# A split last PV, a maximum taken away inside PSUM and spare matmuls in the tail of a fused attention and soft-MoE kernel

## The chip, the cores and the metric

The kernel runs on one core of a Trainium2 chip. The metric is the device time in microseconds of one execution; of the runs of a kernel the median counts. A profile belongs to one execution and has a span, from the first to the last recorded instruction, that is a little shorter than that execution's time.

## What is computed

Two stages follow each other. The first is attention with a choice of key chunks, for 4 batches, 8 heads, 768 positions and a head width of 64:

```
ub   = sum_d max(q * k_min[chunk], q * k_max[chunk])    # 24 chunks of 32 keys, causal
sel  = the 6 chunks of each query with the largest ub
attn = softmax(q k^T / 8 over chosen, causal keys);  x = attn v     # -> [3072, 512]
```

The second is a soft mixture of experts over all 3072 tokens, with 8 experts of 4 slots each (32 slots):

```
logits = x phi
d = softmax of logits over the tokens;  slot_input = d^T x
slot_out[e] = relu(slot_input[e] w1[e]) w2[e]           # w1: 512 x 1024, w2: 1024 x 512
c = softmax of logits over the slots;   out = c slot_out
```

## The kernel before

**Work and order.** The order of the instructions on each engine is written out by hand. A loop over `i` goes through 16 pairs of heads, four pairs to a batch, in a software pipeline: in turn `i` it makes scores and exponentials of pair `i` (`scores`, `expo`, six groups of key blocks), chooses chunks for pair `i + 1`, loads and transposes pairs ahead, multiplies probabilities with values for pair `i - 1` (`pv`, in parts `[0, 1, 2]`, `[3]`, `[4]`, `[5]`, one number for each tile of 128 queries), and normalises and transposes the result of pair `i - 2` (`normalise`, `x_transposes`, `evac_x`). `expo` runs ScalarE's exponential (L289) and then a mask select on GpSimd (POOL, L291).

**The MoE part beside it.** When a batch's four pairs are through, `moe_logits` multiplies the transposed x with phi, `moe_copy` and `moe_max` take the largest logit of each slot over the tokens, `moe_bound` and `moe_exp` bring it to all partitions and take it away, and the running maximum `m_run` and the running sums `si_acc` are corrected by `dm`. `moe_comb` makes the softmax over the slots (`c_pad`), `moe_dispatch` the slot inputs (`si`), and `moe_ct` transposes `c`.

**Weights.** The 16 blocks of expert weights, 1 MB each, are loaded by GpSimd's queue (`load_w`, L120) in the turns that `wplan` (L456 to L461) names: none in turns 2, 5, 8 and 11, two in 12 and 13, one elsewhere. Values of pair `i + 2` (L132) stand just ahead of them in the queue, mask selects just behind.

**The tail.** Behind the loop come L546 to L677. PV of the last pair is done as `[0, 1, 2, 3]` and `[4, 5]`, into two tiles of the pool `p_sc`, and normalised in the same two pieces (L549 to L562); the pair's x is copied out by ScalarE for the first piece and by VectorE for the second. The logits of the last batch are accumulated in one PSUM tile, three quarters of the width before the last pair is ready, one quarter after it. `moe_copy` (L360) reduces them to `pm`, L370 transposes that, L377 reduces it to `mb`, L383 brings it to all partitions by a product with the identity in float32, L390 to L392 make the new maximum and subtract it, L396 takes the exponential, L427 is dispatch. L580 and L587 put the sums into the padded expert input `siT_pad` and the normaliser row `zrow`. `experts_in` (L605) and `experts_out` (L640) run four experts at once in four column groups of TensorE, `relu` and `hidden_T` stand between them. `normalisers` (L623 to L631) makes 24 column sums of `c` and the slot normaliser, between the halves of `experts_out`. L657 scales the expert output into `so_sb`. Then 24 tiles of output are made (L668), copied in turn by VectorE (L670) and ScalarE (L672), and written by SyncE's queue in pairs of tiles; the first and the last pair are written tile by tile.

**Pools of PSUM.** `p_sc` and `p_tp` have two buffers each, `p_at` one; a tile waits until the earlier user of its buffer has been read.

Of the kernel before, what the change touches and what calls it, by code (L numbers as in the profile page):

```python
# [46 lines left out]
def kernel(  # L47
# [247 lines left out]
        st["e", i, g] = e  # L295

    def pv(i, ts):
        if i == LAST and ts[0] in (0, 4):
            st["at", i] = p_sc.tile([P, 2, 512], F32, name="at_ps", tag="sc")
        elif ts[0] == 0:  # L300
            st["at", i] = p_at.tile([P, 2, 512], F32, name="at_ps", tag="at")
        at = st["at", i]
        for t in ts:
            for h in range(2):
                o = at[:, h, t * (D + 1):(t + 1) * (D + 1)]
                for kg in range(t + 1):
                    g, c = BLOCK[(kg, t)]
                    nc.tensor.matmul(  # L308
                        o, lhsT=st["e", i, g][:, h, c:c + P], rhs=v_t[i % NV][:, h, kg, :],
                        start=(kg == 0), stop=(kg == t),  # L310
                    )

    def normalise(i, t0=0, t1=NQT, at=None):
        b, j = divmod(i, NPB)
        at = st.pop(("at", i)) if at is None else at
        at = at[:, :, :NQT * (D + 1)].rearrange("p h (t d) -> p h t d", t=NQT)[:, :, t0:t1]
# [21 lines left out]
    def evac_x(i, t0=0, t1=NQT, copy=nc.vector.tensor_copy):  # L338
        b, j = divmod(i, NPB)
        ps = st.pop(("xTps", i, t0))  # L340
        copy(st["xT", b][:, j, t0 * P:t1 * P], ps[:, t0:t1].rearrange("p t c -> p (t c)"))


    def moe_logits(b, hgs=range(NDG), home=(p_tp, "tp")):
        if hgs[0] == 0:
            st["lgps", b] = home[0].tile([P, NQT, NS], F32, name="lg_ps", tag=home[1])
        ps, xT = st["lgps", b], st["xT", b]
        for t in range(NQT):
            for hg in hgs:
                nc.tensor.matmul(  # L350
                    ps[:, t, :], lhsT=xT[:, hg, t * P:(t + 1) * P], rhs=phi_sb[:, hg, :],
                    start=(hg == 0 and t == 0), stop=(hg == NDG - 1 and t == NQT - 1),
                )

    def moe_copy(b):
        lg = small.tile([P, NQT, NS], F32, name="lg", tag="lg")
        pm = small.tile([P, NS], F32, name="pm", tag="pm")
        ps = st.pop(("lgps", b))
        if b == B - 1:
            nc.vector.tensor_reduce(pm, ps.rearrange("p t s -> p s t"), axis=AX.X, op=ALU.max)  # L360
            nc.scalar.copy(lg, ps)
        else:
            nc.vector.tensor_copy(lg, ps)
            nc.vector.tensor_reduce(pm, lg.rearrange("p t s -> p s t"), axis=AX.X, op=ALU.max)
        st["lg", b], st["pm", b] = lg, pm

    def moe_max(b):
# [12 lines left out]
    def moe_exp(b):  # L380
        lg = st["lg", b]
        bc = p_tp.tile([P, NS], F32, name="bc_ps", tag="tp")
        nc.tensor.matmul(  # L383
            bc, lhsT=st.pop(("mb", b)).broadcast_to([NS, P]), rhs=identf[:NS, :NS], start=True, stop=True,
        )
# [10 lines left out]
        nc.scalar.activation(d_sb, ld, func=ACT.Exp)  # L396
        st["d", b] = d_sb
        if b > 0:

            dm = small.tile([P, 1, NS], F32, name="dm", tag="dm")  # L400
            nc.vector.tensor_tensor(dm[:, 0, :], m_old, m_new, op=ALU.subtract)
            nc.scalar.activation(dm, dm, func=ACT.Exp)
            if b == B - 1:
                moe_comb(b)
# [42 lines left out]
    def have(i):  # L447
        return 0 <= i < NPAIR
# [5 lines left out]


    wplan = {i: 1 for i in range(-1, NPAIR)}  # L456
    for i in (2, 5, 8, 11):
        wplan[i] = 0
    for i in (12, 13):
        wplan[i] = 2  # L460
    nw = 1  # L461

    def weights(i):
# [5 lines left out]
    for i in range(-2, NPAIR):  # L469
# [34 lines left out]
        if have(i - 2):  # L504
            x_transposes(i - 2)
        if have(i - 1):
            pv(i - 1, [3])
        if have(i + 2):
            transposes(i + 2, "q")
            evac_T(i + 2, "q")  # L510
# [10 lines left out]
        if have(i):  # L521
            scores(i, 4)
            expo(i, 4)
            scores(i, 5)
            expo(i, 5)
        if have(i + 1) and i >= 0:
            ns_transposes(i + 1)
            evac_ns(i + 1)
        if have(i - 1):
            pv(i - 1, [4])  # L530
        moe(moe_dispatch, i - 3)
        if have(i - 1):
            pv(i - 1, [5])
        if have(i + 2):
            qsplit(i + 2)
# [10 lines left out]
    pads = ctx.enter_context(tc.tile_pool(name="pads", bufs=1))  # L546
    siT_pad = pads.tile([P, NDG, E, CH], BF16, name="siT_pad")
    hT_pad = pads.tile([P, NFG, E, CH], BF16, name="hT_pad")
    normalise(LAST - 1)  # L549
    pv(LAST, [0, 1, 2, 3])  # L550
    at_a = st["at", LAST]
    x_transposes(LAST - 1)
    evac_x(LAST - 1, copy=nc.scalar.copy)
    normalise(LAST, 0, 4, at_a)
    pv(LAST, [4, 5])
    moe_logits(B - 1, range(NDG - 1), (p_at, "at"))
    x_transposes(LAST, 0, 4)
    evac_x(LAST, 0, 4, nc.scalar.copy)
    normalise(LAST, 4, NQT)
    x_transposes(LAST, 4, NQT)  # L560
    evac_x(LAST, 4, NQT)
    moe_logits(B - 1, range(NDG - 1, NDG))  # L562
    nc.gpsimd.memset(siT_pad, 0.0)
    nc.gpsimd.memset(hT_pad, 0.0)
    i_ctx.close()
    moe_copy(B - 1)
    moe_max(B - 1)
    moe_bound(B - 1)
    moe_exp(B - 1)
    moe_dispatch(B - 1)  # L570


    tail = ctx.enter_context(tc.tile_pool(name="tail", bufs=1))
# [11 lines left out]
    for g in range(2):  # L585
# [6 lines left out]
    moe_ct(B - 1)  # L592
# [30 lines left out]
    def normalisers():  # L623
        ps = p_tp.tile([P, B * NQT + 1], F32, name="cs_ps", tag="tp")
        for n in range(B * NQT):
            nc.tensor.matmul(
                ps[:, n:n + 1], lhsT=cT[:, n // 2, n % 2], rhs=ones_sq[:, :1], start=True, stop=True)
        nc.tensor.matmul(
            ps[:, B * NQT:], lhsT=zrow.rearrange("p j s -> p (j s)"), rhs=identf[:1, :1], start=True, stop=True)
        nc.vector.reciprocal(zinv, ps[:, B * NQT:])  # L630
        nc.vector.reciprocal(cinv, ps[:, :B * NQT])  # L631

    so_ps = p_at.tile([P, 2, 512], F32, name="so_ps", tag="at")

    def experts_out(f):
        for g in range(2):
            for fg in range(f * 4, (f + 1) * 4):
                for j in range(4):
                    e = g * 4 + j
                    nc.tensor.matmul(  # L640
                        so_ps[j * CH:(j + 1) * CH, 0, :], lhsT=hT_pad[:, fg, e, :],
                        rhs=w_sb[E + e][:, fg * Dm:(fg + 1) * Dm],
                        start=(g == 0 and fg == 0), stop=(g == 1 and fg == NFG - 1),
                    )

    experts_in(0, 0)
    experts_in(0, 1)
    relu(0)
    experts_in(1, 0)
    hidden_T(0)  # L650
    experts_in(1, 1)
    relu(1)
    experts_out(0)
    hidden_T(1)
    normalisers()
    experts_out(1)
    nc.scalar.activation(so_sb, so_ps[:, 0, :], func=ACT.Copy, scale=zinv)  # L657


# [2 lines left out]
    for m in range(B * NQT // 2):  # L662
        o_sb = op.tile([P, 2, Dm], F32, name="o_sb", tag="o_sb")
        rows = out[m * 2 * P:(m + 1) * 2 * P, :].rearrange("(p x) d -> p x d", x=2)
        for x in range(2):
            pool, tag = homes[n % 5]
            o_ps = pool.tile([P, Dm], F32, name="o_ps", tag=tag)
            nc.tensor.matmul(o_ps, lhsT=cT[:, m, x], rhs=so_sb, start=True, stop=True)  # L668
            if x == 0:
                nc.vector.tensor_scalar_mul(o_sb[:, x, :], o_ps, cinv[:, n:n + 1])  # L670
            else:
                nc.scalar.activation(o_sb[:, x, :], o_ps, func=ACT.Copy, scale=cinv[:, n:n + 1])  # L672
# [35 lines left out]
```

## Time and profile before

| what | value |
|---|---|
| three runs | 177.64, 177.72, 176.17 us; median 177.64 |
| the profiled execution | 177.53 us, span 175.8 |
| busy: TensorE, VectorE, ScalarE, GpSimd | 139.1, 128.8, 120.0, 99.9 us |
| weight blocks, issue to landing | 12.9 us median; the last is issued at 129.11 and lands 18.9 us later |
| output transfers | 6.29 MB through SyncE's queue, 14 issues |

In the page, section 2 cuts the span into 40 slices; a digit is the busy share in tenths, and `PEclk` is the clock that TensorE was granted, in tenths of full. The chain of work that ended last is followed back from the last instruction, each step to what released it. In the timeline a row gives start, length, engine, line, operation, tiles, shape, count, and in brackets the idle time before it and what ended it. PEld is the weight load that belongs to a matmul and can run ahead of it.

### The profile page before, as it was taken

The page shows a single profiled execution, that of the slowest core. Times are in us where ns is not written, and L with a number is a line of the kernel's source. Part 1 is how long each engine was busy: PE and PEld are TensorE (multiplying, and loading weights), DVE is VectorE, ACT ScalarE, POOL GpSimd, SP SyncE. Part 2 cuts the span into 40 slices and gives each one's busy share as a digit, 9 for nine tenths or more (in the row PEclk, how much of TensorE's full clock was granted, in tenths as well). Part 3 has the DMA queues.
Part 4 walks back from the last instruction along what each step waited for, and adds up shares of the span by engine and source line. Part 5 has one row for each costly group of instructions (what it writes and reads, how often), then busy time and mean ns, then how long its engine had stood idle before and what let it go on. Part 6 is the DMA issues. An engine that isn't in the chain of part 4 may idle for free.

```text
span 175.8 us, 5994 instructions
## 1 busy us (share of the span) xinstructions
PE 139.1 (79%) x2486; PEld 95.9 (55%) x2486; DVE 128.8 (73%) x429; ACT 120.0 (68%) x163; POOL 99.9 (57%) x194
## 2 busy tenths in 40 slices
PE   0449888999889889999988999999689569986500
PEld 0334556777567657766765776677467444532000
DVE  4456979999889998999998999999752650246530
ACT  2336798989789778988977698897667321156430
POOL 7995679869768557877775585759344600000000
PEclk9999999999999999999999999999999956999755
DMA  3999999999999999999999999199999993009995
GB/s 50 167 158 180 194 206 200 206 197 209 179 212 193 215 185 143 200 172 203 172 147 203 169 207 141 17 187 211 200 214 214 213 215 72 4 13 403 402 405 212
DMA packets 40460, 32.92 MB, mean 187 GB/s; under 512 B 26353, under 2 KB 34545, under 8 KB 40433
## 3 DMA queue, kind: packets, MB, share of 16 engines
q0 software_dynamic: 38416, 26.25, 101.8%
q1 hardware_dynamic: 2016, 6.29, 9.1%
q8 instruction: 19, 0.31, 0.7%
q14 instruction: 9, 0.07, 0.1%
HBM read 52.49 MB, written 6.29 MB: 334 GB/s over the span
## 4 chain that ended last, share of the span: by engine, by line
PE 36%; ACT 19%; DVE 13%; DMA 12%; POOL 11%; issue 5%; POOLq 0%; DVEq 0%; ACTq 0%
ACT e_sb L289 13%; DMA k_in<-in_k_dram 7%; PE sc_ps L271 6%; DMA out_dram<-o_sb 5%; PE at_ps L308 5%; PE sc_ps L277 4%; PE tr_ps L184 3%; PE h_ps L605 3%; DVE x_sb L321 3%; POOL e_sb L291 3%; POOL q_in L127 2%; PE ns_ps L253 2%; POOL k_in L127 2%; PE so_ps L640 2%; PE si_ps L427 2%
## 5 line engine op out<-in xcount | busy, mean ns | idle before, releaser
L289 ACT ACTIVATE e_sb<-sc_ps 128x1024 bf16<-128x1024 f32 x96 | 83.6, 936 | 10.9 <-PE sc_ps L277 9.9
L291 POOL TENSOR_SCALAR_AFFINE_SELECT e_sb<-e_sb 128x256 bf16<-128x256 bf16 x96 | 39.5, 423 | 32.7 <-ACT e_sb L289 32.0
L271 PE MATMUL sc_ps<-qT,kT 64*128 64x512 bf16 (+3 forms) x256 | 39.6, 310 | 6.6 <-ACT e_sb L289 6.3
L277 PE MATMUL sc_ps<-nsT,smask 64*128 64x512 bf16 (+3 forms) x256 | 36.8, 306 | 0.0
L308 PE MATMUL at_ps<-v_t,e_sb 128*128 128x65 bf16 x672 | 29.4, 194 | 1.2 <-DVE x_sb L321 1.1
L308 PEld LDWEIGHTS <-e_sb 128*128 128x128 bf16 x672 | 25.1, 98 | 3.4 <-DVE x_sb L321 1.6
L271 PEld LDWEIGHTS <-kT 64*128 64x128 bf16 x256 | 15.8, 94 | 16.8 <-issue 8.7
L242 DVE MAX8 mx<-ub_ps 128x8 f32<-128x24 f32 x192 | 18.8, 170 | 4.6 <-PE ub_ps L231 4.5
L202 DVE TENSOR_REDUCE mm<-kT 128x24 bf16<-128x768 bf16 x16 | 15.2, 949 | 4.0 <-ACT kT L193 4.0
L132 POOL DMA_DIRECT2D v_t<-in_v_dram x16 | 16.7, 1042 | 1.9 <-PE ns_ps L253 1.2
L193 ACT COPY kT<-tr_ps 128x768 bf16<-128x768 bf16 x16 | 12.8, 803 | 6.5 <-PE tr_ps L184 6.5
L321 DVE TENSOR_TENSOR x_sb<-at_ps,inv 128x768 bf16<-128x768 f32 (+2 forms) x17 | 15.5, 910 | 0.6
L277 PEld LDWEIGHTS <-smask 64*128 64x128 bf16 x256 | 13.1, 95 | 4.4 <-issue 0.3
L208 DVE TENSOR_REDUCE mm<-kT 128x24 bf16<-128x768 bf16 x16 | 15.1, 942 | 0.0
L193 ACT COPY qT<-tr_ps 128x768 bf16<-128x768 bf16 x16 | 13.2, 825 | 2.7 <-PE tr_ps L184 2.7
L184 PE MATMUL tr_ps<-ident,k_in 128*64 128x128 bf16 x192 | 9.2, 237 | 6.6 <-DMA k_in<-in_k_dram 5.5
L670 DVE TENSOR_SCALAR o_sb<-o_ps,cinv 128x512 f32<-128x512 f32 x12 | 8.6, 748 | 7.2 <-PE o_ps L668 4.1
L231 PE MATMUL ub_ps<-bd,qpn 128*128 128x48 bf16 x192 | 10.4, 187 | 2.8 <-DVE qpn L218 2.5
L127 POOL DMA_DIRECT2D k_in<-in_k_dram x16 | 11.7, 729 | 1.3 <-POOLq L692 0.8
L261 DVE COPY nsT<-ns_ps 128x768 bf16<-128x768 bf16 x16 | 8.9, 556 | 4.0 <-PE ns_ps L253 3.5
L672 ACT ACTIVATE o_sb<-o_ps,cinv 128x512 f32<-128x512 f32 x12 | 7.8, 688 | 5.7 <-DMA out_dram<-o_sb 3.8
L127 POOL DMA_DIRECT2D q_in<-in_q_dram x16 | 11.5, 721 | 0.0
(95 smaller groups left out, 213.2 us busy)
## 6 DMA issues: line engine op xcount, KB each, us to landing
w_sb<-in_moe_w_dram POOLq DMA_DIRECT2D x16, 1024.0 KB, 12.9
out_dram<-o_sb SPq DMA_DIRECT2D x10, 512.0 KB, 5.5
k_in<-in_k_dram POOLq DMA_DIRECT2D x16, 192.0 KB, 7.9
q_in<-in_q_dram POOLq DMA_DIRECT2D x16, 192.0 KB, 8.1
v_t<-in_v_dram POOLq DMA_DIRECT2D x16, 192.0 KB, 9.3
out_dram<-o_sb SPq DMA_DIRECT2D x4, 256.0 KB, 3.4
phi_sb<-in_moe_phi_dram POOLq DMA_DIRECT2D x1, 32.0 KB, 9.6
```

What stands on the lines that cost most here:

```text
L127: nc.gpsimd.dma_start(out=t, in_=src.rearrange("h (p g) d -> p h (g d)", p=P))
L132: nc.gpsimd.dma_start(out=v_t[i % NV][:, :, :, :D], in_=v[b, 2 * j:2 * j + 2].rearrange("h (g p) d -> p h g d", p=P),)
L193: nc.scalar.copy(t.rearrange("d (p g) -> d p g", g=NQT), st.pop((nm + "ps", i)).rearrange("d g p -> d p g"),)
L202: nc.vector.tensor_reduce(mm[:, 0, 0, :], kT, axis=AX.X, op=ALU.min)
L208: nc.vector.tensor_reduce(mm[:, 1, 0, :], kT, axis=AX.X, op=ALU.max)
L242: nc.vector.max(mx[:, a, :], ub[:, a, :])
L271: nc.tensor.matmul(ps[:, h, c:c + w], lhsT=kT[r, kg * P:(kg + 1) * P], rhs=qT[r, qs], start=True, stop=False,)
L277: nc.tensor.matmul(ps[:, h, c:c + w], lhsT=smask[r, kg].rearrange("p a b -> p (a b)"), rhs=nsT[r, qs], start=False, stop=True,)
L289: nc.scalar.activation(e[:, :, :w], st.pop(("scps", i, g))[:, :, :w], func=ACT.Exp, scale=scale)
L291: nc.gpsimd.affine_select(out=e[:, :, :P], in_=e[:, :, :P], compare_op=ALU.is_ge, fill=0.0, base=0, pattern=[[0, 2], [1, P]], channel_mult ...
L308: nc.tensor.matmul(o, lhsT=st["e", i, g][:, h, c:c + P], rhs=v_t[i % NV][:, h, kg, :], start=(kg == 0), stop=(kg == t),)
L321: nc.vector.tensor_tensor(st["x", b][:, t0:t1, 2 * j:2 * j + 2, :].rearrange("p t h d -> p h t d"), at[:, :, :, :D], inv.broadcast_to([P, ...
```

## The change

It touches only the last turn of the loop, the tail, and the place of one weight load.

1. In the last turn, PV of pair 14 is done as `[3, 4]` ahead of score group 4, and `[5]` between groups 4 and 5. PV of pair 15 is cut into `[0, 1, 2]` (a tile of `p_tp`) and `[3]`, `[4, 5]` (a tile of `p_sc`), and normalised, transposed and copied in pieces of three tiles.
2. The last batch's logits are computed twice, into `lg1` and `lg2`. From `lg1` the slot maximum is taken, together with the earlier maximum, which a one-column matmul puts beside the transposed `pm`; the reduction gives the negative. A float32 matmul adds it into `lg2` in PSUM, and the exponential reads that. `m_new`, the copy `lg` and the subtraction `ld` are gone.
3. `keep(n)` issues `n` matmuls of 512 columns whose result nobody reads, into the half of the logits tile that `lg1` does not use; six in all, at four places.
4. `moe_ct` of the last batch stands behind the first 16 expert matmuls. `experts_out` runs its first half in two parts around `hidden_T(1)`; `zsum` takes the slot normaliser, and `csums` takes the 24 column sums behind the last expert matmul.
5. The first output tile is made by two matmuls of 256 columns, one half copied by VectorE and one by ScalarE.
6. `wplan` names a block in turn 11 and one instead of two in turn 13.

The diff, cut to its core:

```diff
     def pv(i, ts):
-        if i == LAST and ts[0] in (0, 4):
+        if i == LAST and ts[0] == 0:
+            st["at", i] = p_tp.tile([P, 2, 3 * (D + 1)], F32, name="at_ps", tag="tp")
+        elif i == LAST and ts[0] == 3:
             st["at", i] = p_sc.tile([P, 2, 512], F32, name="at_ps", tag="sc")
...
-    for i in (2, 5, 8, 11):
+    for i in (2, 5, 8):
         wplan[i] = 0
-    for i in (12, 13):
-        wplan[i] = 2
+    wplan[12] = 2
...
-            pv(i - 1, [3])
+            pv(i - 1, [3] if i < LAST else [3, 4])
...
             expo(i, 4)
+            if i == LAST:
+                pv(i - 1, [5])
             scores(i, 5)
...
-    pv(LAST, [0, 1, 2, 3])
+    pv(LAST, [0, 1, 2])
     at_a = st["at", LAST]
+    pv(LAST, [3])
+    at_b = st["at", LAST]
     x_transposes(LAST - 1)
     evac_x(LAST - 1, copy=nc.scalar.copy)
-    normalise(LAST, 0, 4, at_a)
+    normalise(LAST, 0, 3, at_a)
     pv(LAST, [4, 5])
-    moe_logits(B - 1, range(NDG - 1), (p_at, "at"))
-    x_transposes(LAST, 0, 4)
-    evac_x(LAST, 0, 4, nc.scalar.copy)
-    normalise(LAST, 4, NQT)
-    x_transposes(LAST, 4, NQT)
-    evac_x(LAST, 4, NQT)
-    moe_logits(B - 1, range(NDG - 1, NDG))
+    lgt = p_at.tile([P, 2, 512], F32, name="lgt_ps", tag="at")
+    lg1 = lgt[:, 0, :NQT * NS].rearrange("p (t s) -> p t s", t=NQT)
+    def keep(n):
+        for _ in range(n):
+            nc.tensor.matmul(lgt[:, 1, :], lhsT=ident, rhs=w_sb[0][:, :512], start=True, stop=True)
+    moe_logits(BL, range(NDG - 1), lg1)
+    x_transposes(LAST, 0, 3)
+    evac_x(LAST, 0, 3, nc.scalar.copy)
+    normalise(LAST, 3, NQT, at_b)
+    lg2 = p_sc.tile([P, 2, 512], F32, name="lg2_ps", tag="sc")[:, 0, :NQT * NS].rearrange("p (t s) -> p t s", t=NQT)
+    moe_logits(BL, range(NDG - 1), lg2, False)
+    x_transposes(LAST, 3, NQT)
+    evac_x(LAST, 3, NQT)
+    keep(2)
+    moe_logits(BL, range(NDG - 1, NDG), lg1)
...
-    moe_copy(B - 1)
-    moe_max(B - 1)
-    moe_bound(B - 1)
-    moe_exp(B - 1)
-    moe_dispatch(B - 1)
+    nc.vector.tensor_reduce(pm, lg1.rearrange("p t s -> p s t"), axis=AX.X, op=ALU.max)
+    moe_logits(BL, range(NDG - 1, NDG), lg2, False)
+    pmT = p_tp.tile([NS, P + 1], F32, name="pmT_ps", tag="tp")
+    nc.tensor.matmul(pmT[:, P:], lhsT=m_old[:1, :], rhs=identf[:1, :1], start=True, stop=True)
+    keep(1)
+    nc.tensor.matmul(pmT[:, :P], lhsT=pm, rhs=identf, is_transpose=True)
+    nc.vector.tensor_reduce(mneg, pmT, axis=AX.X, op=ALU.max, negate=True)
+    keep(2)
+    nc.tensor.matmul(
+        lg2, lhsT=mneg.broadcast_to([NS, P]), rhs=rep.broadcast_to([NS, NQT, NS]), start=False, stop=True,
+    )
+    nc.tensor.matmul(bc, lhsT=mneg.broadcast_to([NS, P]), rhs=identf[:NS, :NS], start=True, stop=True)
+    nc.scalar.activation(d_sb, lg2, func=ACT.Exp)
+    nc.vector.tensor_reduce(rm, lg1, axis=AX.X, op=ALU.max)
+    nc.vector.tensor_tensor(dm[:, 0, :], m_old, bc, op=ALU.add)
+    nc.scalar.activation(dm, dm, func=ACT.Exp)
+    nc.vector.tensor_tensor(lc, lg1, rm.broadcast_to([P, NQT, NS]), op=ALU.subtract)
+    nc.vector.tensor_tensor(si_acc, si_acc, dm.broadcast_to([P, NDG + 1, NS]), op=ALU.mult)
...
+    keep(1)
+    moe_dispatch(BL)
...
     experts_in(0, 0)
+    moe_ct(B - 1)
     experts_in(0, 1)
     relu(0)
     experts_in(1, 0)
     hidden_T(0)
     experts_in(1, 1)
     relu(1)
-    experts_out(0)
+    experts_out(0, [0])
     hidden_T(1)
-    normalisers()
-    experts_out(1)
+    zsum()
+    experts_out(0, [1])
+    experts_out(1, [0, 1])
+    csums()
...
+            if n == 0:
+                o_ps = pool.tile([P, 2, Dm], F32, name="o2_ps", tag=tag)
+                for y in range(2):
+                    nc.tensor.matmul(
+                        o_ps[:, y, :256], lhsT=cT[:, m, x], rhs=so_sb[:, y * 256:(y + 1) * 256],
+                        start=True, stop=True,
+                    )
+                nc.vector.tensor_scalar_mul(o_sb[:, x, :256], o_ps[:, 0, :256], cinv[:, :1])
+                nc.scalar.activation(o_sb[:, x, 256:], o_ps[:, 1, :256], func=ACT.Copy, scale=cinv[:, :1])
```

More of the change, by code (lines that the diff above doesn't have):

```diff
@@ L301, in pv @@
             st["at", i] = p_at.tile([P, 2, 512], F32, name="at_ps", tag="at")
-        at = st["at", i]
+        at, tb = st["at", i], 3 if i == LAST and ts[0] > 2 else 0
         for t in ts:
             for h in range(2):
-                o = at[:, h, t * (D + 1):(t + 1) * (D + 1)]
+                o = at[:, h, (t - tb) * (D + 1):(t - tb + 1) * (D + 1)]
                 for kg in range(t + 1):
@@ L315, in normalise @@
         at = st.pop(("at", i)) if at is None else at
-        at = at[:, :, :NQT * (D + 1)].rearrange("p h (t d) -> p h t d", t=NQT)[:, :, t0:t1]
+        at = at[:, :, :(t1 - t0) * (D + 1)].rearrange("p h (t d) -> p h t d", t=t1 - t0)
         if j == 0:
@@ L341, in evac_x, with moe_logits @@
         copy(st["xT", b][:, j, t0 * P:t1 * P], ps[:, t0:t1].rearrange("p t c -> p (t c)"))
[L344 to L347, printed above, removed]
+    def moe_logits(b, hgs=range(NDG), ps=None, last=True):
+        if ps is None:
+            ps = st["lgps", b] = p_tp.tile([P, NQT, NS], F32, name="lg_ps", tag="tp")
+        xT = st["xT", b]
         for t in range(NQT):
@@ L351, in moe_logits @@
                     ps[:, t, :], lhsT=xT[:, hg, t * P:(t + 1) * P], rhs=phi_sb[:, hg, :],
-                    start=(hg == 0 and t == 0), stop=(hg == NDG - 1 and t == NQT - 1),
+                    start=(hg == 0 and t == 0), stop=(last and hg == NDG - 1 and t == NQT - 1),
                 )
@@ L357, in moe_copy @@
         pm = small.tile([P, NS], F32, name="pm", tag="pm")
[L358 to L364, printed above, removed]
+        nc.vector.tensor_copy(lg, st.pop(("lgps", b)))
+        nc.vector.tensor_reduce(pm, lg.rearrange("p t s -> p s t"), axis=AX.X, op=ALU.max)
         st["lg", b], st["pm", b] = lg, pm
@@ L402, in moe_exp @@
             nc.scalar.activation(dm, dm, func=ACT.Exp)
-            if b == B - 1:
-                moe_comb(b)
             nc.vector.tensor_tensor(si_acc, si_acc, dm.broadcast_to([P, NDG + 1, NS]), op=ALU.mult)
@@ L528 @@
             evac_ns(i + 1)
-        if have(i - 1):
+        if have(i - 1) and i < LAST:
             pv(i - 1, [4])
         moe(moe_dispatch, i - 3)
-        if have(i - 1):
+        if have(i - 1) and i < LAST:
             pv(i - 1, [5])
@@ L548 @@
     hT_pad = pads.tile([P, NFG, E, CH], BF16, name="hT_pad")
+    BL = B - 1
     normalise(LAST - 1)
-    pv(LAST, [0, 1, 2, 3])
+    pv(LAST, [0, 1, 2])
     at_a = st["at", LAST]
+    pv(LAST, [3])
+    at_b = st["at", LAST]
     x_transposes(LAST - 1)
     evac_x(LAST - 1, copy=nc.scalar.copy)
-    normalise(LAST, 0, 4, at_a)
+    normalise(LAST, 0, 3, at_a)
     pv(LAST, [4, 5])
-    moe_logits(B - 1, range(NDG - 1), (p_at, "at"))
-    x_transposes(LAST, 0, 4)
-    evac_x(LAST, 0, 4, nc.scalar.copy)
-    normalise(LAST, 4, NQT)
-    x_transposes(LAST, 4, NQT)
-    evac_x(LAST, 4, NQT)
-    moe_logits(B - 1, range(NDG - 1, NDG))
+    lgt = p_at.tile([P, 2, 512], F32, name="lgt_ps", tag="at")
[13 more added lines that the diff above has]
+    moe_logits(BL, range(NDG - 1, NDG), lg1)
     nc.gpsimd.memset(siT_pad, 0.0)
@@ L565 @@
     i_ctx.close()
-    moe_copy(B - 1)
-    moe_max(B - 1)
-    moe_bound(B - 1)
-    moe_exp(B - 1)
-    moe_dispatch(B - 1)
-    tail = ctx.enter_context(tc.tile_pool(name="tail", bufs=1))
+    tail = ctx.enter_context(tc.tile_pool(name="tail", bufs=1))
+    m_old = m_run[(BL + 1) % 2]
+    pm = small.tile([P, NS], F32, name="pm", tag="pm")
+    nc.vector.tensor_reduce(pm, lg1.rearrange("p t s -> p s t"), axis=AX.X, op=ALU.max)
[4 more added lines that the diff above has]
+    nc.tensor.matmul(pmT[:, :P], lhsT=pm, rhs=identf, is_transpose=True)
+    mneg = small.tile([NS, 1], F32, name="mb", tag="mb")
+    nc.vector.tensor_reduce(mneg, pmT, axis=AX.X, op=ALU.max, negate=True)
+    keep(2)
+    rep = identf[:NS, :NS].rearrange("p (o s) -> p o s", o=1)
+    nc.tensor.matmul(
+        lg2, lhsT=mneg.broadcast_to([NS, P]), rhs=rep.broadcast_to([NS, NQT, NS]), start=False, stop=True,
+    )
+    bc = p_tp.tile([P, NS], F32, name="bc_ps", tag="tp")
+    nc.tensor.matmul(
+        bc, lhsT=mneg.broadcast_to([NS, P]), rhs=identf[:NS, :NS], start=True, stop=True,
+    )
+    d_sb = small.tile([P, NQT, NS], BF16, name="d_sb", tag="d_sb")
+    nc.scalar.activation(d_sb, lg2, func=ACT.Exp)
+    st["d", BL] = d_sb
+    rm = small.tile([P, NQT, 1], F32, name="rm", tag="rm")
+    nc.vector.tensor_reduce(rm, lg1, axis=AX.X, op=ALU.max)
+    dm = small.tile([P, 1, NS], F32, name="dm", tag="dm")
+    nc.vector.tensor_tensor(dm[:, 0, :], m_old, bc, op=ALU.add)
+    nc.scalar.activation(dm, dm, func=ACT.Exp)
+    lc = small.tile([P, NQT, NS], F32, name="lc", tag="lc")
+    nc.vector.tensor_tensor(lc, lg1, rm.broadcast_to([P, NQT, NS]), op=ALU.subtract)
+    nc.vector.tensor_tensor(si_acc, si_acc, dm.broadcast_to([P, NDG + 1, NS]), op=ALU.mult)
+    for g in range(2):
+        nc.scalar.activation(
+            c_pad[:, :, :, g * SPE:(g + 1) * SPE],
+            lc[:, :, g * 16:(g + 1) * 16].rearrange("p t (j s) -> p t j s", j=4), func=ACT.Exp,
+        )
+    keep(1)
+    moe_dispatch(BL)
     op = ctx.enter_context(tc.tile_pool(name="op", bufs=5))
@@ L591 @@
         )
-    moe_ct(B - 1)
     cinv = tail.tile([P, B * NQT], F32, name="cinv")
@@ L621, in hidden_T, with zsum, csums @@
             nc.vector.tensor_copy(o, i_)
-    def normalisers():
-        ps = p_tp.tile([P, B * NQT + 1], F32, name="cs_ps", tag="tp")
+    def zsum():
+        ps = p_tp.tile([P, 1], F32, name="z_ps", tag="tp")
+        nc.tensor.matmul(
+            ps, lhsT=zrow.rearrange("p j s -> p (j s)"), rhs=identf[:1, :1], start=True, stop=True)
+        nc.vector.reciprocal(zinv, ps)
+    def csums():
+        ps = p_tp.tile([P, B * NQT], F32, name="cs_ps", tag="tp")
         for n in range(B * NQT):
@@ L627, in normalisers, with experts_out @@
                 ps[:, n:n + 1], lhsT=cT[:, n // 2, n % 2], rhs=ones_sq[:, :1], start=True, stop=True)
[L628 to L631, printed above, removed]
+        nc.vector.reciprocal(cinv, ps)
     so_ps = p_at.tile([P, 2, 512], F32, name="so_ps", tag="at")
-    def experts_out(f):
-        for g in range(2):
+    def experts_out(f, gs):
+        for g in gs:
             for fg in range(f * 4, (f + 1) * 4):
@@ L666 @@
             pool, tag = homes[n % 5]
-            o_ps = pool.tile([P, Dm], F32, name="o_ps", tag=tag)
-            nc.tensor.matmul(o_ps, lhsT=cT[:, m, x], rhs=so_sb, start=True, stop=True)
-            if x == 0:
+            if n == 0:
+                o_ps = pool.tile([P, 2, Dm], F32, name="o2_ps", tag=tag)
+                for y in range(2):
+                    nc.tensor.matmul(
+                        o_ps[:, y, :256], lhsT=cT[:, m, x], rhs=so_sb[:, y * 256:(y + 1) * 256],
+                        start=True, stop=True,
+                    )
+                nc.vector.tensor_scalar_mul(o_sb[:, x, :256], o_ps[:, 0, :256], cinv[:, :1])
+                nc.scalar.activation(o_sb[:, x, 256:], o_ps[:, 1, :256], func=ACT.Copy, scale=cinv[:, :1])
+            else:
+                o_ps = pool.tile([P, Dm], F32, name="o_ps", tag=tag)
+                nc.tensor.matmul(o_ps, lhsT=cT[:, m, x], rhs=so_sb, start=True, stop=True)
+            if n == 0:
+                pass
+            elif x == 0:
                 nc.vector.tensor_scalar_mul(o_sb[:, x, :], o_ps, cinv[:, n:n + 1])
```

## The prediction, made before the change was run

> **What bounds the kernel now.** I read the page first, then the chain that ended last from 130 us on, then the timeline of that stretch, then TensorE alone in stretches of 3.41 us. The page:
>
> ```profile
> span 175.8 us, 5994 instructions
> ...
> PEclk9999999999999999999999999999999956999755
> DMA  3999999999999999999999999199999993009995
> ```
>
> Until about 134 us three engines are full, and the change touches nothing there but the place of a weight load. From 134 to 157 us the program is a thread of single steps. From 158 us on the DMA engines are full with the output (9 in nearly every slice), so the end lies a fixed time behind the first output transfer: what the thread gains up to there is gained at the end. The chain:
>
> ```profile
> 137.50 0.81 ACT xT_sb L341
> ...
> 139.18 0.59 ACT xT_sb L341
> ...
> 140.18 0.37 DVE pm L360
> ...
> 140.59 0.30 PE pmT_ps L370
> ...
> 140.91 0.29 DVE mb L377
> ...
> 141.25 0.65 PE bc_ps L383 x2
> ...
> 142.60 0.37 ACT d_sb L396
> ...
> 143.01 0.96 PE si_ps L427 x30
> ...
> 144.75 4.27 PE h_ps L605 x33
> ...
> 152.42 0.58 PE cs_ps L626 x24
> ...
> 155.20 0.70 ACT so_sb L657
> ...
> 156.56 1.59 ACT o_sb L672 x3
> 158.16 3.11 DMA out_dram<-o_sb
> ```
>
> The reader is to see start, duration and what ran: nothing overlaps, and 33 expert matmuls take 4.27 us, while the 32 of L640 take 1.90 in the timeline. The cause is the granted clock (columns: stretch, length, TensorE busy and count, clock, DMA share, GB/s):
>
> ```profile
> 137.62:141.03 3.41, 2.09 (x48) 1.00 1.06 215
> 141.03:144.44 3.41, 2.06 (x38) 0.51 1.06 215
> 144.44:147.86 3.42, 3.42 (x35) 0.50 0.65 131
> 147.86:151.27 3.41, 3.41 (x64) 1.00 0.02 5
> ...
> 161.51:164.92 3.41, 1.24 (x5) 1.00 1.02 404
> 164.92:168.33 3.41, 1.47 (x3) 0.51 1.03 404
> ```
>
> The clock halves near 141.05, returns near 147.9 and halves again near 164.95: 2 and 5 steps of 3.41 us apart. Before both falls lies a step with little streaming.
>
> **The change, part by part** (times of the profiled execution; minus is a gain).
>
> *Last PV split, a: -0.41 at pm.* The last two tiles of pair 14 now stand ahead of score groups 4 and 5, so its PV ends about 0.64 sooner: 12 PV matmuls at 0.036 each (22 in 0.79 us of weight loads) after the scores of group 4, instead of 22 after group 5. They push those scores back by 10 x 0.036 = 0.36; ScalarE was busy until 134.49 anyway, so its exponential starts only some 0.13 later. Normalise, transposes and ScalarE's copy of pair 14 follow 0.64 sooner. Then three transposes and a 384-wide copy (0.48, by the slope from 0.80 for 768 to 0.59 for 512; 0.40 at least, 0.59 at most) stand where four and 512 stood. VectorE's copy of the other half becomes the later one: 0.36 (between 0.29 for 256 and 0.56 for 768) behind 18 new logits matmuls at 0.025 (24 in 0.75, less one drain) = 0.45 on the path. The two spare matmuls (0.43) lie beside that copy. After it three logits matmuls instead of six: 0.08. Together pm starts at 139.77 instead of 140.18. Bounds: -0.7 (the 18 matmuls hidden) and 0.
>
> *Slot maximum in PSUM: -0.09.* Gone: m_run 0.20 and ld 0.36, with their hand-overs, 0.66 between bc's end and d_sb's start. Added: a two-pass f32 matmul with 192 columns. The nearest rows are
>
> ```profile
> 122.93 0.40 PE L383 MATMUL bc_ps<-identf,mb 32*128 32x32 f32 x2
> ...
> 155.94 1.24 PE L668 MATMUL o_ps<-so_sb,cT_all 128*128 128x512 bf16 x5 [0.79 <-ACT so_sb L657]
> ```
>
> so 0.40 at full clock if columns cost nothing, 0.67 if each of the 160 further columns takes, in two passes, twice the 0.216/512 of the second row; I take 0.55. But two spare matmuls write the tile that lg1 lies in, and the built program gives each a wait on VectorE. One stands between pm and its transpose: it cannot start before pm ends, 0.21 more (0.216 each, from that second row). The other stands ahead of dispatch and waits for lc, which stands behind rm and dm on VectorE, and dm behind the second f32 product. From the end of mb: dm at +0.80, lc +0.90 to +1.26, spare +1.30, dispatch +1.51, although d_sb is ready at +1.02. Before, dispatch came at 143.01 - 141.20 = +1.81. The one-column matmul for the old maximum (0.26 at most, as L628's) runs beside pm's reduction. So -0.30 + 0.21 = -0.09, bounds -0.6 (waits short) and +0.4 (f32 at 0.67, late lc). Queued behind that spare are all 30 dispatch matmuls.
>
> *Dispatch to experts: -0.47.* Dispatch to siT_pad takes 1.06 at half clock; at full clock the same 30 took 0.94 (127.94 to 128.88). The first 16 expert matmuls now wait only for siT_pad's first half, 0.22 + 0.04, while cT stood ahead of them until 144.68. So 1.20 against 1.67. The six cT transposes come back later: +0.34 (the weight loads of 129.04).
>
> *Expert input: -1.63.* Sixty-four matmuls from 144.68 to 150.17 are 5.49. At full clock four take 0.22 (16 from 149.29 to 150.17), so 64 take 3.52, plus 0.34 for the hidden transposes: 3.86. This needs the clock to stay. By columns, without transposes, at 0.216 per 512: the step up to 141.03 held about 12 x 65 and 24 x 32 columns, 0.65 us, and fell; 161.51 to 164.92 held about 0.86 and fell; 123.97 to 127.38 held about 0.96 and stayed at 1.00. The changed kernel has about 48 x 32 columns and five spares, 1.73, then the f32 product, one spare, dispatch and the first experts, about 1.5. Bounds 0 (falls as before) and -1.63; nearer to the second by these counts.
>
> The Trainium skill, "TensorE: Matmul & The Clock Gate", Part 1, says that the clock is watched in free-running windows of 3.4 us and halves after an idle one. The grid agrees with the steps above, but the step that fell here was 2.09 us busy, which the page's word "idle" would not have dropped: by the page the clock needed no filling, by the rows it did. The same page says that the grid's place varies from run to run, which would fit the 176.17 among the three times; no run here shows it. By the page's wording alone the spares would bring nothing, and the sum would be near 175.8.
>
> *Column sums beside the last copy: -0.68.* The 24 matmuls (weight loads 0.70 from 152.20, pitch 0.68 in all) go from the thread to the place beside so_sb, 0.69 on ScalarE. Then cinv's reciprocal (0.29) ends about when the first output product does; if that cover fails, at most 0.3. zsum stays on the path, 0.30 as now.
>
> *First output in halves: -0.37.* Now 155.94 to 157.19 from product to issue, 0.75 of it VectorE's copy. Halves: two products of 256 (0.27 long, 0.11 apart), ScalarE from +0.41 for 0.40 (its 128x256 row), issue at +0.88. The second tile's copy starts later on ScalarE, its transfer about when the first (256 KB at 402 GB/s, 0.65) ends. Bounds -0.37 and 0.
>
> *Weight blocks sooner: 0.* POOL issues the blocks of turns 12 and 13 (0.70 each) up to a turn earlier: past the six mask selects, the cast (L244) and the value load of that turn, which wait 0.70 more in turn 11 and 0.70 less in turn 13. Nobody is late by it: turns with and without a block both last 6.85 us (casts at 71.13 and 77.98, at 102.48 and 109.33). No transfer ran near 111 us, so the queue ends some 4 us sooner. The last block landed at 129.11 + 18.9 = 148.0; it is needed near 149.4 by my times, so even unmoved it would hold, by 1.4.
>
> **Sum:** 0.41 + 0.09 + 0.47 - 0.34 + 1.63 + 0.68 + 0.37 = 3.31. The profiled execution took 177.53 (span 175.8 and 1.73 around it), 0.11 under the median of 177.64; 177.53 - 3.31 = 174.2.
>
> **Rivals.** *The clock falls anyway.* For it: 2.09 us busy did not hold it. Against: the column counts. It would then return at the same 147.9, as the grid does not move with the program: dispatch near 143.1, cT 0.7 at half clock, 6.4 groups of four by 147.9, the other 9.6 and the transposes in 2.45, so the second expert product starts near 150.3 as now. Left are 0.68 + 0.37 less 0.13: 176.6. *New waits eat the front.* The two VectorE waits and the 18 logits matmuls at their worse bounds, 0.41 + 0.49: 175.1. For it: both waits stand in the built program. Against: VectorE is otherwise idle. *Slower: the clock is down one step longer.* Place: 147.86 to 151.27; price half a step, 1.7, on top of the first rival: 178.3. It ends above now once more than 1.9 us behind 147.86 run at half clock. Against: the step 144.44 to 147.86, all expert matmuls, lifted it.
>
> **The numbers.** Chances: forecast 0.72, waits 0.09, clock falls 0.14, a step longer 0.05. The forecast's own range is 173.2 to 175.1: down by the good bounds of the split (0.29), of the maximum (0.51) and of the two 384-wide copies (0.15), up by the second rival. The range 173.2 to 176.2 reaches on towards the clock's fall and leaves out that and the last case, 0.19. About 1% is what a measurement here can tell from no change: 175.9 to 179.4. The first two cases and a little of the third are faster, 0.82; the rest of the third and most of the fourth within, 0.15; 0.03 for a fourth worse than priced.
>
> **What would show it.** Clock 1.00 from 134 to 156 us; L644 in fours of 0.22; pm near 139.8; the two spares starting just after pm and lc; no cs_ps between two L682 blocks; first output issue near 153.9. A clock of 0.50 anywhere in 141 to 148 would break the forecast, as would dispatch later than 143.

## The result, and the profile after

The changed kernel took 176.16 us (median of 20 runs, 175.36 to 178.07), the kernel before 176.91 (median of 20, 175.96 to 177.92): a ratio of 0.9955, 95% interval 0.9935 to 0.9974. It is 0.45% faster, which is within the 1% that the prediction called the same, where 1.9% had been forecast. The time itself falls just inside the range, at its slow end; the change was 0.75 us instead of 3.3.

The profiled execution of the changed kernel took 176.21. Its page, of which the fence shows the span, the granted clock, the DMA share and the queue that loads instructions:

```profile
span 174.5 us, 6059 instructions
...
PEclk9999969999999999999999999999999999999655
DMA  3999999999999999999999999999999970029993
...
q8 instruction: 20, 0.33, 0.7%
```

The clock no longer falls where it fell before (the 5 and the 6 in slices 33 and 34 are gone), and the output starts earlier. But the page before has 19 packets in the queue of instructions, this one has 20. The chain that ended last, with start, duration and what ran:

```profile
139.93 0.37 DVE pm L578
140.29 0.04 issue
140.34 0.38 PE lgt_ps L560
...
142.06 0.36 DVE lc L604
142.42 0.04 issue
142.47 0.38 PE lgt_ps L560
142.84 0.76 PE si_ps L422 x30
...
143.95 1.05 PE h_ps L644 x16
145.00 0.44 PE cT_ps L436 x6
145.44 1.84 PE h_ps L644 x32
...
152.88 0.70 ACT so_sb L702
...
154.03 0.49 DVE o_sb L719
154.53 0.02 issue
154.55 0.48 ACT o_sb L720
```

Two spare matmuls (L560) are links of the chain, each behind a VectorE instruction, and so are two half copies of the first output tile, one after the other. Point by point, in the two profiled executions:

| stretch | before | forecast | after |
|---|---|---|---|
| first PV of pair 14 in turn 15 (the marker below) | 131.35 | 131.35 | 131.54 |
| marker to pm | 8.83 | 8.42 | 8.39 |
| pm to the first dispatch matmul | 2.83 | 2.74 | 2.75 |
| dispatch to the first expert matmul | 1.67 | 1.20 | 1.27 |
| to the first so_ps matmul (L682) | 5.49 | 4.20 | 4.48 |
| to the copy so_sb | 5.03 | 4.35 | 4.45 |
| to the first output product | 0.74 | 0.74 | 0.74 |
| to the first output issue | 1.25 | 0.88 | 1.49 |
| that issue comes at | 157.19 | 153.88 | 155.11 |
| first to last packet of output | 16.38 | 16.38 | 17.16 |

So the first issue came 2.08 sooner, and 0.78 of it was lost behind it. Where it was lost shows in the last steps of 1 us (columns: stretch, length, clock, DMA share, GB/s), first of before, then of after:

```profile
172.00:173.00 1.00, 0.50 1.01 387
173.00:174.00 1.00, 0.50 0.75 291
174.00:175.00 1.00, 0.50 0.03 10
```

```profile
170.00:171.00 1.00, 0.50 0.99 377
171.00:172.00 1.00, 0.50 0.69 270
172.00:173.00 1.00, 0.50 0.09 35
173.00:174.00 1.00, 0.50 0.01 2
```

Before, all DMA engines end within about a microsecond of each other; after, most end by 171.9, and two, then one, are still at work up to 173.14. In the trace the twentieth packet of instructions (16 KB, 0.93 us) runs on one DMA engine at 159.92, inside the output; the engines still at work after 171.9 fit that: what was queued behind the packet ends later by about its length. Whether it does is for the experiments.

### The profile page after: what moved, and what is told of

Same layout as the page of the kernel before. It is cut to its first block, busy times and chain, and to the rows that moved or that the text cites. A ratio compares the mean times of both kernels' runs of the same rounds, so it can differ in the third digit from the quotient of the medians.

```text
span 174.5 us, 6059 instructions
## 1 busy us (share of the span) xinstructions
PE 140.4 (80%) x2519; PEld 97.0 (56%) x2521; DVE 128.2 (73%) x427; ACT 120.2 (69%) x163; POOL 99.6 (57%) x194
## 4 chain that ended last, share of the span: by engine, by line
PE 39%; ACT 21%; POOL 14%; DVE 12%; issue 5%; DMA 4%; SPq 0%; POOLq 0%; DVEq 0%; ACTq 0%
ACT e_sb L289 16%; PE sc_ps L271 7%; PE sc_ps L277 5%; PE at_ps L310 5%; POOL e_sb L291 4%; DMA out_dram<-o_sb 4%; PE tr_ps L184 3%; POOL q_in L127 3%; POOL k_in L127 3%; DVE x_sb L323 2%; PE ns_ps L253 2%; PE h_ps L644 2%; PE ub_ps L231 2%; PE so_ps L682 2%; PE si_ps L422 2%
## 5 line engine op out<-in xcount | busy, mean ns | idle before, releaser
L310 PE MATMUL at_ps<-v_t,e_sb 128*128 128x65 bf16 x672 | 30.2, 194 | 1.5 <-DVE x_sb L323 1.1
L271 PEld LDWEIGHTS <-kT 64*128 64x128 bf16 x256 | 15.6, 94 | 16.3 <-issue 8.2
L323 DVE TENSOR_TENSOR x_sb<-at_ps,inv 128x768 bf16<-128x768 f32 (+1 forms) x17 | 15.5, 910 | 0.6
L727 DVE TENSOR_SCALAR o_sb<-o_ps,cinv 128x512 f32<-128x512 f32 x11 | 8.1, 749 | 5.6 <-DMA out_dram<-o_sb 3.4
L723 PE MATMUL o_ps<-so_sb,cT_all 128*128 128x512 bf16 x22 | 7.7, 429 | 4.8 <-DVE o_sb L727 4.3
```

The costliest lines, as they stand in the source:

```text
L271: nc.tensor.matmul(ps[:, h, c:c + w], lhsT=kT[r, kg * P:(kg + 1) * P], rhs=qT[r, qs], start=True, stop=False,)
L310: nc.tensor.matmul(o, lhsT=st["e", i, g][:, h, c:c + P], rhs=v_t[i % NV][:, h, kg, :], start=(kg == 0), stop=(kg == t),)
L323: nc.vector.tensor_tensor(st["x", b][:, t0:t1, 2 * j:2 * j + 2, :].rearrange("p t h d -> p h t d"), at[:, :, :, :D], inv.broadcast_to([P, ...
```

## The experiments

Two accounts of the missing gain were set against each other. The first: the thread came forward nearly as forecast, and three things took it back (the packet of instructions, the waits of the spares, the two halves of the first tile). The second: the parts are simply worth less than the forecast's sizes, the spares above all, and the output's end has a limit of its own. The expectations call an account "theory A" in each case anew and say what it is.

Each kernel is timed against the kernel before on the same chip; the interval belongs to that ratio, which is not exactly the quotient of the two medians (for before_pad 1.0039 against 1.0024). The marker is the start of the first PV matmuls of pair 14 in turn 15. What lies ahead of it differs from execution to execution (131.02 to 132.14 in the profiles, whatever the kernel), so "from the marker" (span less marker, one profiled execution) is the finer number for what happens in the tail; it is 144.45 before and 142.96 after. The page gives the span to 0.1, so it is good to about 0.05.

**no_spare**: the six spare matmuls left out.

```diff
     def keep(n):
-        for _ in range(n):
+        for _ in range(0):
```

> The changed kernel without its six spare matmuls (nobody reads their results). Theory A (the spares hold the clock): the step of 3.41 us up to about 141 us holds only some 0.65 us of streamed columns again, the clock falls to 0.50 for one or two steps between 139 and 148 us, the experts' fours of 0.22 become 0.43, and the time rises from 176.16 to between 176.6 and 177.4; the two waits on VectorE go at the same time, which gives back 0.5 at most. Theory B (the spares only cost): clock 1.00 throughout, dispatch 0.4 to 0.6 sooner, time 175.6.

176.16 us, ratio 0.9967 (0.9936 to 0.9998): the same median as the changed kernel. The clock was 0.50 from 143.58 to 146.99, cT took 0.75 and the first 16 expert matmuls 1.90; the output, with no 16 KB packet of instructions in it, took 16.43. From the marker it is 142.96, as for the changed kernel. So neither theory came out: against the changed kernel, pm to dispatch took 0.62 less and the output 0.73 less, but the first expert matmul to the first so_ps matmul 1.38 more. The held clock is worth there about what comes with the spares: their two waits and, in this build, the packet in the output. The next four kernels take these apart.

**code_pad**: 40 matmuls of one column at the start of the program, which nobody reads.

```diff
+        if i == -1:
+            spare = p_at.tile([P, 2, 512], F32, name="spare_ps", tag="at")
+            for _ in range(40):
+                nc.tensor.matmul(spare[:, 0, :1], lhsT=ident, rhs=ident[:, :1], start=True, stop=True)
```

> The changed kernel with 40 matmuls of one column added in an early idle stretch of TensorE (near 7 us), whose results nobody reads. Theory A (TensorE's instructions are fetched in 16 KB pieces on one DMA engine, and the change, with 64 more of them, moved a further fetch into the output stage, at 159.9 us, which holds that one engine 0.93 us and with it the last output packets): 80 more instructions move the last fetch ahead of the output stage, the output's packets end within 0.6 us of each other instead of 1.3, span 0.6 to 0.8 shorter, time 175.4. Theory B (the late end of the last packets is chance): nothing moves but the start, time 176.2 or up to 0.3 more.

175.43, ratio 0.991 (0.9877 to 0.9943), from the marker 142.18. More instructions, and 0.7 us faster than the changed kernel: the last packet of instructions came at 151.46, ahead of the output, which took 16.42.

**before_pad**: the same edit, with 34 matmuls, to the kernel before.

> The kernel before with 34 one-column matmuls (68 instructions of TensorE) in the idle stretch near 7 us, whose results nobody reads; nothing else is changed. Theory A (a 16 KB fetch of TensorE's instructions inside the output stage costs 0.8 us): the program is now as long as the changed one, the last such fetch falls between 158 and 166 us, the output stage takes 17.2 us instead of 16.4 from its first packet to its last, time 0.7 above the kernel before (ratio 1.004). Theory B (the long output stage belongs to the change itself): output stage 16.4, time as before.

177.69 against 177.26, ratio 1.0039 (1.0008 to 1.007). Here the padding moved a packet into the output, at 162.02 for 0.96 us, and the output took 17.24 instead of 16.38. So the kernel before can be made to pay the same price, with nothing else changed: it belongs to the place of the packet, not to the shorter thread.

**own_tile**: the six spares write to a PSUM tile of their own and not beside lg1.

```diff
-    keep(2)
+    sp = p_sc.tile([P, 2, 512], F32, name="sp_ps", tag="sc")
+    keep(2, sp)
...
-    keep(1)
+    keep(1, sp)
...
```

> The changed kernel with the six spare matmuls writing to a tile of their own instead of the unused half of the logits tile. Theory A (two of the spares wait for VectorE's reads of that tile, and the transpose of pm and the dispatch stand behind them): pm to its transpose 0.2 sooner, dispatch no longer behind lc, so dispatch to follow the end of mb by about 1.1 instead of 1.54 us, together 0.6 us, time 175.5. Theory B (dispatch is held by something else, d_sb or TensorE itself): dispatch within 0.2 us of where it was, time 176.0 to 176.2.

175.26, ratio 0.9889 (0.9852 to 0.9925), from the marker 142.35. The end of mb to dispatch is 1.12 instead of 1.54, pm's start to mb's start 0.73 instead of 0.93: the two waits on VectorE cost 0.62 in this trace.

**own_pad**: own_tile with the 40 matmuls of code_pad.

> The changed kernel with both repairs: the spares in a tile of their own, and 40 one-column matmuls early so that the last instruction fetch lies ahead of the output stage. Theory A (the two losses are separate and add): 0.9 from the one and 0.7 from the other, 174.5. Theory B (both act through the same place, for instance the clock): 175.2, as with one of them.

174.81, ratio 0.9878 (0.984 to 0.9916), from the marker 141.64, output 16.41: in the traces the two repairs add up, -0.71 from the marker against own_tile and -1.32 against the changed kernel. The times alone don't show it: the ratio lies well inside own_tile's interval, and 174.81 lies between the two theories.

**one_copy**: the first output tile as one product and one VectorE copy, as before.

> The changed kernel with its first output tile made by one matmul and copied whole by VectorE, as before. Theory A (the halves run one after the other, because ScalarE's copy waits for VectorE's into the same tile): from the first output product to the first output issue 1.25 us instead of 1.49, the second tile's copy no longer pushed back, first issue 0.2 to 0.5 sooner, time 175.8 or so. Theory B (the halves help, and the loss lies elsewhere): first issue 0.3 later, time 176.4.

176.72, ratio 0.996 (0.9925 to 0.9996). From product to issue it took 1.25 instead of 1.49, as expected of the copy. The time tells nothing of it: in the profiled execution the clock fell, at 144.03, although all six spares were there, and the 16 KB packet was in the output again. In the row of the changed kernel's timeline the bracket names what ScalarE's half waited for:

```profile
154.55 0.48 ACT L720 ACTIVATE o_sb<-o_ps,cinv 128x256 f32<-128x256 f32 x1 [0.99 <-DVE o_sb L719]
```

It waited for VectorE's half. The two copies share the tile that they write, `o_sb`, and the PSUM tile that they read. The kernel before has a case of each kind, first two rows with a shared `o_sb` alone, then two with a shared PSUM tile alone:

```profile
156.35 0.75 DVE L670 TENSOR_SCALAR o_sb<-o_ps,cinv 128x512 f32<-128x512 f32 x1 [2.64 <-PE o_ps L668]
156.56 0.69 ACT L672 ACTIVATE o_sb<-o_ps,cinv 128x512 f32<-128x512 f32 x1 [0.68 <-PE o_ps L668]
```

```profile
140.18 0.36 DVE L360 TENSOR_REDUCE pm<-lg_ps 128x32 f32<-128x192 f32 x1 [0.59 <-PE lg_ps L350]
140.57 0.32 ACT L361 COPY lg<-lg_ps 128x192 f32<-128x192 f32 x1 [0.80 <-DVE pm L360]
```

The two engines filled the two rows of one `o_sb` tile at the same time, but ScalarE's read of `lg_ps` began only when VectorE's had ended, though both only read. So the theory's tile is not the likely one: it is the shared PSUM tile that fits all these rows. No run tries the halves with two PSUM tiles.

**before_spares**: the kernel before, with nothing but six spares in a tile of their own.

```diff
+    sp = p_sc.tile([P, 2, 512], F32, name="sp_ps", tag="sc")
...
     moe_copy(B - 1)
+    keep(1)
     moe_max(B - 1)
+    keep(1)
     moe_bound(B - 1)
     moe_exp(B - 1)
+    keep(4)
```

> The kernel before with six spare matmuls alone, into a tile of their own: one beside pm, one beside mb, four behind the product that spreads the maximum. Theory A (spares can hold the clock, and its fall costs the kernel before 1 to 1.6 us in its middle execution): clock 1.00 through the experts in most executions, time 175.4 to 176.0. Theory B (spares hold nothing; whether the clock falls depends on where its steps of 3.41 us lie): time as before, 176.9 to 177.3, with the same spread of 2 us.

175.23 (175.03 to 175.55), ratio 0.9902 (0.9867 to 0.9937), from the marker 142.31. One part of the change alone, with other places for the spares, gives more than the whole, and the six runs lie within 0.5 us of each other, where the 17 of the kernel before spread over 1.9. What the rest of the change brings is lost again in it.

**own_sub**: own_tile without the second set of logits; VectorE subtracts the maximum (`ld`, as before), three spares instead of one ahead of dispatch, and the first output tile is copied whole.

```diff
-    moe_logits(BL, range(NDG - 1), lg2, False)
...
-    moe_logits(BL, range(NDG - 1, NDG), lg2, False)
...
-    nc.tensor.matmul(
-        lg2, lhsT=mneg.broadcast_to([NS, P]), rhs=rep.broadcast_to([NS, NQT, NS]), start=False, stop=True,
-    )
...
+    nc.vector.tensor_tensor(
+        ld, lg, bc.rearrange("p (o s) -> p o s", o=1).broadcast_to([P, NQT, NS]), op=ALU.add,
+    )
```

> The changed kernel with the spares in a tile of their own, one set of logits, the maximum subtracted by VectorE (so no subtraction in PSUM and no second set of 24 logits matmuls), the first output tile copied whole; 47 TensorE instructions fewer, so no fetch should fall in the output stage. Theory A (the second set costs as much as the subtraction in PSUM saves): mb to dispatch 1.3 instead of 1.0 us, the last transposes of x 0.44 sooner, and with the shorter program and the whole copy 174.3. Theory B (the subtraction in PSUM is worth its price): 0.3 or more above the version with both repairs, 174.9.

174.34, ratio 0.9849 (0.9811 to 0.9888), from the marker 141.28. Marker to pm is 8.06 instead of 8.39, so the 24 further logits matmuls cost 0.33; the end of mb to dispatch is 1.37 instead of own_tile's 1.12, so the addition in PSUM saves 0.25. The two nearly cancel.

**ct_first**: own_sub with the transposes of c where they stood before.

```diff
+    moe_ct(B - 1)
     experts_in(0, 0)
-    moe_ct(B - 1)
```

> own_sub with the last batch's six transposes of c (moe_ct) back ahead of the first 16 expert matmuls, as in the kernel before. Theory A: in that place they run while TensorE waits for siT_pad anyway (143.43 to 143.94 in before_spares, 5.28 from dispatch to the first so_ps matmul against 5.75 in own_sub), so dispatch to the first so_ps matmul falls from 5.75 to about 5.3 and the time by 0.45: about 173.9, ratio about 0.982. Theory B, my forecast's sizes: the move behind the first experts was worth 0.47 - 0.34 = 0.13, so undoing it costs 0.1: 174.4 to 174.5, ratio 0.985 to 0.986.

173.56, ratio 0.9817 (0.9782 to 0.9853), from the marker 140.79: 0.49 less than own_sub, so moving them had cost, and had not gained. The chain of own_sub, and then that of ct_first:

```profile
142.06 0.92 PE si_ps L422 x30
143.01 0.04 issue
143.06 0.23 DVE siT_pad L620
143.33 1.05 PE h_ps L644 x16
144.38 0.44 PE cT_ps L436 x6
144.82 1.84 PE h_ps L644 x32
```

```profile
142.45 0.90 PE si_ps L422 x30
143.36 0.51 PE cT_ps L436 x6
143.87 2.70 PE h_ps L644 x48
```

In own_sub TensorE stands still from 142.98 to 143.33 until siT_pad is there, and transposes c later; in ct_first the transposes fill that gap and 48 matmuls follow without a break: dispatch to the first expert matmul takes 1.35 instead of 1.27, from there to the first so_ps matmul 3.92 instead of 4.48. This is the fastest version: 3.5 us below the kernel before on the same chip (177.11), and it needs neither the second logits nor the halves.

**csums_mid**: own_sub with the column sums ahead of the last 32 expert matmuls.

```diff
+    csums()
     experts_out(1, [0, 1])
-    csums()
```

> own_sub with the 24 column sums of c ahead of the last 32 expert matmuls, no longer beside the copy so_sb. Theory A, the forecast's term: they lie on the thread again, +0.68, so about 175.0, ratio about 0.989; the first so_sb copy comes 0.68 later after the first so_ps matmul. Rival: at full clock they are hidden by the wait for hT_pad there, or cinv's reciprocal was late for the first copy: the time moves by less than 0.3.

174.54, ratio 0.9866 (0.9834 to 0.9898), from the marker 141.94, 0.66 more than own_sub; from the first so_ps matmul to so_sb 5.25 instead of 4.45. So the trace has them on the thread at about the forecast's price. The medians differ by 0.2 only, less than the intervals can tell, so the time alone would not have settled it.

**late_block**: own_sub with the weight blocks in the turns of the kernel before.

```diff
-    for i in (2, 5, 8):
+    for i in (2, 5, 8, 11):
         wplan[i] = 0
-    wplan[12] = 2
+    for i in (12, 13):
+        wplan[i] = 2
```

> own_sub with the weight blocks in the turns of the kernel before (none in turn 11, two in turns 12 and 13). Theory A, the forecast's term: 0, the last block lands near 148.0 and its user, the second half of the first so_ps sum, comes near 148.7; ratio 0.985. Rival: the thread is now faster by 1.4 than in the kernel before, and the block is late for it: so_ps stretched by up to 0.5 behind the block's landing, ratio up to 0.988.

174.45, ratio 0.9856 (0.9822 to 0.9889), from the marker 141.17; dispatch to the first so_ps of the chain is 5.93 in both. The block's place costs nothing, in either turn.

**pv14_late**: own_sub with PV of pair 14 in its old places in the last turn.

```diff
-            pv(i - 1, [3] if i < LAST else [3, 4])
+            pv(i - 1, [3])
...
-            if i == LAST:
-                pv(i - 1, [5])
...
-        if have(i - 1) and i < LAST:
+        if have(i - 1):
             pv(i - 1, [4])
...
```

> own_sub with PV of pair 14 in the last turn in its old places: tile 3, then score groups 4 and 5, then tiles 4 and 5. Pair 15's split stays. Theory A, the forecast's working: normalise and transposes of pair 14 come 0.64 later, the last exponentials 0.13 sooner, and of the measured 0.44 at pm 0.2 to 0.5 is lost, so the time is 174.6 to 174.9. Rival: the gain at pm comes from the split of pair 15 alone, and pm stays within 0.1 of own_sub's.

175.12, ratio 0.9878 (0.9842 to 0.9914), from the marker 141.86. Marker to pm is 8.76 instead of 8.06, so the earlier PV of pair 14 is worth 0.70, more than the 0.2 to 0.5 expected. And 8.76 is only 0.07 under the 8.83 of before: cutting pair 15 into three and three tiles, with two spares in that stretch, is worth next to nothing.

## Why the prediction was wrong

Three steps of the forecast failed. The first output in halves was to gain 0.37 and cost 0.24. The end did not lie a fixed time behind the first output transfer; 0.78 was lost there. And the sum was taken from an execution 0.62 slower than the median, in which the experts ran at half clock. Smaller is a fourth: the transposes of c cost 0.56 behind the first experts and not 0.34. All the steps, in the forecast's terms:

- *Last PV split, -0.41.* Measured -0.44, but made up otherwise: -0.70 from pair 14, -0.07 from pair 15's cut, +0.33 from the second set of logits.
- *Slot maximum in PSUM, -0.09.* Measured -0.08. Both waits on VectorE came where the built program had put them, and cost 0.62 (own_tile). The forecast had them right.
- *Dispatch to experts, -0.47, and the transposes' +0.34.* The first came to -0.40; the next stretch, which holds the transposes, came out 0.28 longer than forecast. The first was priced against half clock, and there the comparison misled. Once the clock is full, the transposes of c fit into TensorE's wait for siT_pad: moving them behind the experts gains 0.08 there and costs 0.56 in the next stretch, 0.49 from the marker (ct_first). Each was costed against the kernel before as it ran, not against the kernel in which another part of the change had already taken effect.
- *Expert input, -1.63.* Right in mechanism and nearly in size for this execution: the clock stayed at 1.00 from 134 to 162, and at full clock, without the transposes, the stretch of 5.49 takes 3.92 (before_spares, ct_first), where 3.86 was forecast. What misled was the execution it was taken from, which lies 0.62 above the median of 20. With spares and nothing else the kernel before gains 1.0%, about 1.7, where these two profiles differ by 2.14 from the marker: the mean loses less to the clock than that execution.
- *Column sums, -0.68.* Measured -0.58 in the changed kernel; 0.66 by csums_mid. Right.
- *First output in halves, -0.37.* Measured +0.24: wrong in its mechanism. The forecast let ScalarE's half run beside VectorE's, but it started 0.02 after VectorE's had ended, and took 0.48, not 0.40. Of the two tiles that the halves share, the PSUM tile is the likely cause of the wait (one_copy).
- *Weight blocks, 0.* Right (late_block).
- "the end lies a fixed time behind the first output transfer": wrong, by 0.78. A 16 KB packet of instructions came into the output, where the kernel before had its last one ahead of it (150.74); code_pad and before_pad show that its place is the cause.

The gap closes with these. Of the 3.31, 0.62 is what the profiled execution lay above the median, 0.78 went to the instruction packet, 0.61 to the halves (0.24 instead of -0.37), 0.35 to dispatch, experts and transposes, 0.10 to the column sums, and 0.19 to a tail that began later in the profiled execution (why is open: its clock was 0.50 for 3.41 us near 24 us, but the tail of no_spare, without such a step, began later still). That leaves 0.66, against a measured 0.75.

Of the rivals, *new waits eat the front* had the right mechanism, but it was in the forecast's sum already. *The clock falls anyway* did not happen in this execution, but in one_copy's, at 144.03 with all spares there; in no_spare, without them, it fell at 143.58. None of the rivals was a loss behind the thread's end, and there the largest single one lay.

The criterion for the clock, streamed columns in a step of 3.41 us, does not hold. The steps (columns: stretch, length, TensorE busy and count, clock, DMA share, GB/s) of one_copy, which fell, and of before_spares, which did not:

```profile
140.62:144.03 3.41, 2.49 (x43) 1.00 0.55 111
144.03:147.45 3.42, 3.42 (x34) 0.50 0.02 5
```

```profile
137.06:140.48 3.42, 2.25 (x57) 1.00 1.07 216
140.48:143.89 3.41, 3.08 (x48) 1.00 1.06 214
```

Whether a step lost the clock shows in the row behind it. One with TensorE busy for 2.49 lost it, one with 2.25 kept it, and in own_sub one with 1.76 kept it (159.07 to 162.48). By the forecast's count the step that fell held, in three spares (3 x 0.216) and 30 dispatch matmuls (30 x 32 x 0.216/512 = 0.40) alone, 1.05 us of columns, where 0.96 had been enough elsewhere. Neither busy time nor columns, so counted, is what decides; what does stays open, and so does how often the changed kernel loses its clock. Its runs of 177.78 and 178.07, against a median of 176.16, would fit a fall, but those executions have no profile. The Trainium skill, "TensorE: Matmul & The Clock Gate", Part 1, says that the windows run freely and their place varies from run to run. These traces agree: the clock fell near 141.05, at 143.58 and at 144.03 in the profiles of three kernels (before, no_spare, one_copy), times that no one grid of 3.41 us holds. What its word "idle" means is not settled by them: no step that fell here was idle.

## What to carry to other kernels

Cost a change against the other parts of the same change, and against the median of many executions: a stall in one profile can be an accident of where the clock's steps lie. Ask of every two engines that share a tile, even in different halves, whether the program lets them overlap: here a spare matmul waited for VectorE's reads in the other half of its PSUM tile, and ScalarE's copy for VectorE's out of one PSUM tile. A tile of their own for the spares costs a line and was worth 0.6 us. When a transfer-bound stage starts sooner but ends no sooner, look in it for a packet that isn't yours.

## What the runs showed of the hardware

- One packet of 16 KB of instructions, 0.93 to 0.96 us on one of 16 DMA engines, lengthened a 16.4 us output by 0.78 to 0.86 us in the four kernels whose profile had it there (after, one_copy, own_tile, before_pad); in the ten others the output took 16.3 to 16.4. All fourteen have one packet of 8 KB of another instruction queue (0.31 to 0.32 us) in the output, so that one does not tell them apart. The 68 to 80 instructions of 34 or 40 one-column matmuls decided where the larger one fell.
- The runs of the kernel before spread over 2 us (20 runs). Those of the eight kernels with spares in a tile of their own spread over 0.5 to 1.3 (5 or 6 runs each), before_spares least. A part of what looked like noise may be the clock; executions without a profile don't show it.
- Adding a float32 row to 192 columns in PSUM took 0.53 on the chain of the changed kernel; with VectorE's addition in its place the end of mb to dispatch was only 0.25 longer (own_sub against own_tile).
